# Third batch's score visits regrouped into six PSUM banks, and the last tile's output written in two halves, in a fused attention and MLP kernel

## The chip, the cores and the metric

The kernel runs on one core of one Trainium2 chip. The metric is device time in microseconds of one execution. Before the change the median of 3 runs is 351.26 us (351.23 to 351.55).

## What is computed

Causal attention with 16 extra "beacon" keys per head, then a mixer layer. Batch 8, 8 heads, 576 tokens, head size 64, so 512 channels; the MLP is 512 to 2048 to 512, applied to 8 x 576 = 4608 rows.

```python
k_all = concat([beacon_k, k], axis=2); v_all = concat([beacon_v, v], axis=2)
scores = q @ k_all.T / sqrt(D)            # causal over the 576 tokens, the beacons are open to all
a = softmax(scores); x = a @ v_all        # -> (8, 576, 512)
h = x.T @ U @ V                           # rank 32, along the tokens
u = x + h.T
out = u + relu(u @ w_ch1) @ w_ch2
```

## The kernel before

**Units of work.** Attention runs over 32 *pairs* p of heads: batch `b = p // 4`, pair `c = p % 4` in the batch. Pairs 8 to 11 are the third batch (b = 2). The MLP runs over 9 blocks of 512 rows. Matmul operands are fp16.

For one pair these steps are done, each a short run of instructions:

- *regroup* (`regroup`, L268 and L270, called by `regroup_of`, L691): three VectorE copies that bring the loaded keys (`pr0`) and then the queries (`pr1`) of a pair into the layout that the transposes take.
- *transposes* (`qkT_of`, `qkT_units`): six transposes of the queries into one PSUM bank (TensorE, L275), which a VectorE copy takes to `qT` (L308); the same for the keys, with a second small copy for the beacons (L308, L313).
- *score groups*: the causal score matrix (keys on partitions, queries on columns) of one head is cut into four groups of at most 496 columns, each one bank: group 0 has 496 columns, group 1 464, group 2 496 in three matmuls (336, 80, 80), group 3 208. The two heads of a pair use the two halves of TensorE's rows. A *visit* is a run of such matmuls (L348 in `score_units`, L382 in the freer `visit`), followed by ScalarE's exponentials, which empty the banks into `expt` tiles (L354, L388). There are four `expt` tiles, so pairs p and p + 2 share theirs.
- *masks* (`mask_head`): two VectorE operations per head that cut the causal corners of `expt` (L324, L326). They come after the pair's exponentials and before its value products.
- *value products* (`av_unit`): 15 matmuls per head into one bank `po` (L397), then VectorE's reciprocal (L405) and multiply (L406).

The MLP is a queue of units, four TensorE matmuls of 512 columns each: `g_unit` (L534, `gps`, one bank, emptied at once by ScalarE L547 or VectorE L549, by a fixed rule on the unit's number) and `c_unit` (L560, `cps`; four units share a bank, the last one is followed by VectorE's L573 or, in the first block, L575 and L577, and by the output write). `fill(n)` takes n units from the queue.

**Order.** The order of TensorE, ScalarE, VectorE, SP and POOL is written out by hand: each engine runs its instructions in the order in which the program emits them. PSUM has eight banks; `pst` (L105) hands out the bank that was freed longest ago in the order of the program, and `emptying` (L112) puts a bank at the end of that list when its last reader is emitted. A tile so waits for whichever engine empties its bank.

**The stage of the change.** The main loop (L1007) goes over pairs 8 to 31. Pairs 12 to 31 use `long_slot` (L964), whose visits take six banks and run across pair borders. Pairs 8 to 11 use the general order at its end: visit of groups 0 and 1 of the next pair, first value product, query transposes two pairs ahead, visit of groups 2 and 3 of the next pair, its masks, key transposes, second value product, regroup three pairs ahead. `QUOTA` (L748) spreads 4 MLP units over these steps. Ahead of the loop, pair 8 has its own two visits. Together with pair 8's, the loop makes ten visits of four banks for pairs 8 to 12.

**The last tile.** The last 128 rows of the output are computed by `c_piece` (L581): 256 columns in 16 matmuls, then 128, then 128 columns (L589), each with a VectorE add (L594) and a write on SP's queue (L596).

Of the kernel before, what the change touches and what calls it, by code (L numbers as in the profile page):

```python
# [18 lines left out]
P = 128  # L19
# [11 lines left out]
def kernel(  # L31
# [73 lines left out]
    def pst(shape, dtype, name):  # L105

        b = emptied.pop(0)
        t = psum.tile(shape, dtype, tag=f"bank{b}", name=name)
        bank_of[id(t)] = (b, t)
        return t  # L110
# [407 lines left out]
    def mlp_units(t0, n, dst, flip, turned=True, last=False):  # L518


        units = []
        gT = {}
        held = {}

        def turn():
            ut = utp.tile([P, 4, DM], F16, name="ut", tag="ut")
            for cc in range(NCC):
                nc.sync.dma_start_transpose(out=ut[:, :, ts(cc, P)], in_=uT[:, cc, ds(t0, 4 * P)])
            gT["u"] = ut

        def g_part(dc, upto):
            g, done = held.get(dc) or (pst([P, 512], F32, name="gps"), 0)
            for cc in range(done, upto):
                nc.tensor.matmul(  # L534
                    g[:, 0:n], w1[:, cc, ts(dc, P)], uT[:, cc, ds(t0, n)], start=(cc == 0), stop=(cc == NCC - 1)
                )
            held[dc] = g, upto

        def g_unit(dc):
            if dc == 0:  # L540
                gT["t"] = gtp.tile([P, NDC, 512], F16, name="gT", tag="gT")
                if turned:
                    turn()
            g_part(dc, NCC)
            g, _ = held.pop(dc)
            if (dc % 3 if not turned else (dc + flip) % 2 or dc in (5, 6, 7)):
                nc.scalar.activation(out=gT["t"][:, dc, 0:n], in_=g[:, 0:n], func=AF.Relu)  # L547
            else:
                nc.vector.tensor_scalar_max(out=gT["t"][:, dc, 0:n], in0=g[:, 0:n], scalar1=0.0)  # L549
            emptying(g)  # L550

        cps = {}

        def c_unit(i, part):
            m = min(P, n - P * i)
            if part == 0:
                cps["t"] = pst([P, DM], F32, name="cps")
            ps = cps["t"]
            for dc in range(4 * part, 4 * part + 4):
                nc.tensor.matmul(  # L560
                    ps[:m, :], gT["t"][:, dc, ds(P * i, m)], w2[:, dc, :], start=(dc == 0),
                    stop=turned and dc == NDC - 1, skip_group_check=True,
                )
            if part == 3:
                ob = outp.tile([P, DM], F32, name="ob", tag="ob")
                if not turned:
                    for cc in range(NCC):
                        nc.tensor.matmul(
                            ps[:m, ts(cc, P)], uT[:, cc, ds(t0 + P * i, m)], ident, start=False, stop=True,
                            skip_group_check=True,  # L570
                        )
                if turned:
                    nc.vector.tensor_tensor(out=ob[:m, :], in0=ps[:m, :], in1=gT["u"][:m, i, :], op=ALU.add)  # L573
                elif i % 2:
                    nc.scalar.activation(out=ob[:m, :], in_=ps[:m, :], func=AF.Copy)  # L575
                else:
                    nc.vector.tensor_copy(out=ob[:m, :], in_=ps[:m, :])  # L577
                emptying(ps)
                nc.sync.dma_start(out=dst(i, m), in_=ob[:m, :])

        def c_piece(i, part):  # L581

            o, w, d0, d1 = [
                (0, 2 * P, 0, NDC // 2), (0, 2 * P, NDC // 2, NDC), (2 * P, P, 0, NDC), (3 * P, P, 0, NDC)
            ][part]
            if d0 == 0:
                cps["t"] = pst([P, w], F32, name="cph")
            for dc in range(d0, d1):
                nc.tensor.matmul(  # L589
                    cps["t"], gT["t"][:, dc, ts(i, P)], w2[:, dc, ds(o, w)], start=(dc == 0), stop=(dc == NDC - 1)  # L590
                )
            if d1 == NDC:
                ob = outp.tile([P, w], F32, name="oh", tag="ob")
                nc.vector.tensor_tensor(out=ob, in0=cps["t"], in1=gT["u"][:, i, ds(o, w)], op=ALU.add)  # L594
                emptying(cps["t"])
                nc.sync.dma_start(out=dst(i, P)[:, ds(o, w)], in_=ob)  # L596

        units += [lambda dc=dc: g_unit(dc) for dc in range(NDC)]
        for i in range((n + P - 1) // P):
            c = c_piece if last and i == n // P - 1 else c_unit  # L600
            units += [lambda i=i, part=part, c=c: c(i, part) for part in range(4)]
        return units, g_part

# [87 lines left out]
    def regroup_of(p):  # L691
        b, c = divmod(p, NH2)
        prs[p] = [regroup(Ls[b][0], c, i, nc.vector.tensor_copy) for i in range(2)]
# [15 lines left out]
    def qkT_of(p):  # L709
        b, c = divmod(p, NH2)  # L710
        new_qT_of(p)
        copies = [(act_copy, nc.vector.tensor_copy) if p == 0 else (nc.vector.tensor_copy,)] * 2
        turns = by_heads(Ls[b][0], c)
        for i, t in enumerate(prs.get(p, ())):
            if t is not None:
                turns[i] = in_pair(prs[p])[i]
        return qkT_units(turns, qTs[b], kTs[b % 2], c, copies, Ls[0][0][0] if p == 0 else None)
# [4 lines left out]
    def scores_of(p):  # L722
        b, c = divmod(p, NH2)
        return score_units(c, qTs[b], kTs[b % 2], expts_of(p), p in ON_PE)

    def masks_of(p):
        scores_of(p)[2]()

    def av_of(p):
        b, c = divmod(p, NH2)  # L730
        if c == 0:
            xbs[b] = xbp.tile([P, NT, DM], F16, name="xb", tag="xb")
        return [
            lambda i=i: av_unit(b, 2 * c + i, expts[(2 * p + i) % NE], vss[b % 2], xbs[b]) for i in range(2)
        ]


    NF = 2
# [5 lines left out]
    HINT = 5  # L744

    FIRST = [3, 3, 2, 1]

    QUOTA = {2: 4}  # L748

    IDLE = [8, 1, 1, 0, 1]  # L750
    queue = []
# [7 lines left out]
    def fill(n):  # L759
        while n > 0 and queue:  # L760
            u = queue.pop(0)
            if u is not None:
                u()
            n -= 1
# [28 lines left out]
    with tc.manual_schedule(engines={ENG.PE, ENG.Activation, ENG.DVE, ENG.SP, ENG.Pool}):  # L793
# [135 lines left out]
        regroup_of(NP1)  # L929
        regroup_of(NP1 + 1)  # L930
        fill(8)
        t0, sc, t1 = qkT_of(NP1), scores_of(NP1), qkT_of(NP1 + 1)
        for u in t0 + sc[0:1] + t1[0:1] + sc[1:3] + t1[1:2]:
            u()
            fill(1)
        regroup_of(NP1 + 2)
        tr = []


# [10 lines left out]
        def go(parts, mixed=0):  # L950

            parts = [(p, g) for p, g in parts if p < NP]
            if parts:
                visit(parts)
            for u in mixing[:mixed]:
                u()
            del mixing[:mixed]
# [6 lines left out]
        def long_slot(p, c, av, qk):  # L964
# [29 lines left out]
            else:  # L994
# [6 lines left out]
                if p + 1 < NP:  # L1001
# [2 lines left out]
                    masks_of(p + 1)  # L1004
                    fill(1)

        for p in range(NP1, NP):  # L1007
            b, c = divmod(p, NH2)
            if c == (1 if b >= DT0 else 0) and b + 1 < B:
                load_batch(b + 1)  # L1010
            if c == (1 if b + 1 == DT0 else 2) and DT0 <= b + 2 < B:
                load_whole(b + 2)
            sc = scores_of(p + 1) if p < P6 else []
            qk = qkT_of(p + 2) if p + 2 < min(NP, DT0 * NH2) else []
            av = av_of(p) if p < P6 else []
            if c == 0 and DT0 <= b + 1 < B and b != DT0:
                tr = turns(b + 1)
            if c == NH2 - 1 and b + 1 == DT0:
                tr = turns(b + 2)
            if c in (0, NH2 - 1) and b + 1 == DT0:  # L1020
                fill_turns(tr, NT)
            if c == 0 and b > NF and p <= P6:
                (mix if p < P6 else mix_between)(b - 1)
            if c == 0 and b + 1 >= DT0:
                fill_turns(tr, 2 * NT)
            if p >= P6:
                long_slot(p, c, av_of(p), qk or [lambda: None] * 2)
                continue
            seq = sc[0:1] + av[0:1] + qk[0:1] + sc[1:3] + qk[1:2] + av[1:2]
            if p + 3 < min(NP, DT0 * NH2):  # L1030
                seq.append(lambda p=p: regroup_of(p + 3))
            quota = QUOTA.get(b, 9)
            done = 0
            for i, u in enumerate(seq):
                want = quota * (i + 1) // len(seq)
                if p + 1 == P6 and i + 1 == len(seq):
                    fill(want - done)
                    done = want
                u()
                fill(want - done)  # L1040
                done = want
        mix(B - 1)
        guard()

# [106 lines left out]
```

## Time and profile before

| what | value |
|---|---|
| median of 3 runs | 351.26 us |
| the profiled execution's own time | 351.05 us |
| its span, first to last instruction | 349.4 us |
| granted TensorE clock, mean | 0.998 |
| busy TensorE / VectorE / ScalarE / POOL | 98% / 54% / 47% / 28% |
| first visit of pair 8 / first visit of pair 13 | 62.41 us / 93.02 us |
| last matmuls of the last tile | from 341.55 us for 3.55 us |

The profile is of one execution. Times in it count from the span's start. A line number is that of the kernel before; where a helper makes an instruction, it is the helper's. "Idle before, releaser" tells what ended the time in which an engine stood still. Matmuls overlap each other by their pipeline, so a group's listed length is longer than the distance to the next group.

### The profile page before, as it was taken

Reading aid. Unit: us, or ns where it says so; the run is one execution under the profiler, and the core shown is the slowest. Engines: PE = TensorE matmul, PEld = TensorE weight load, DVE = VectorE, ACT = ScalarE, POOL = GpSimd, SP = SyncE. Lnnn points to the kernel's source line nnn. Section 1 sums busy time; section 2 is a strip of 40 time slices with the busy share of each in tenths; the row PEclk is TensorE's granted clock in tenths of the full one; section 3 lists DMA queues with packets and bytes.
Section 4 is the critical chain, followed back from the end, with each engine's and each line's share of the span. In section 5 each row is a group of like instructions: output and inputs, shape, how many; then the busy total and the mean of one; then the engine's idle time right before and its main releaser. Section 6 shows DMA issues by size and latency. Waiting matters only on the chain.

```text
span 349.4 us, 7841 instructions
## 1 busy us (share of the span) xinstructions
PE 342.7 (98%) x3105; PEld 174.1 (50%) x3105; DVE 190.2 (54%) x494; ACT 164.2 (47%) x359; POOL 97.9 (28%) x137
## 2 busy tenths in 40 slices
PE   8999999999999999999999999999999999999995
PEld 4565565455554445545454454445445444444444
DVE  5766865588976554645565455535564643323311
ACT  5967851587831666167524843485335103202400
POOL 8976715327415437401840050000000000000000
PEclk9999999999999999999999999999999999999999
DMA  9999999999997999991999899533121323013011
GB/s 167 134 191 174 171 205 171 226 142 142 105 132 136 171 139 125 152 213 29 127 136 157 174 95 134 138 95 68 62 90 32 61 99 90 2 60 105 18 64 65
DMA packets 146780, 41.89 MB, mean 120 GB/s; under 512 B 131504, under 2 KB 142224, under 8 KB 146736
## 3 DMA queue, kind: packets, MB, share of 16 engines
q0 software_dynamic: 87440, 18.18, 66.8%
q1 hardware_dynamic: 59072, 22.84, 37.0%
q8 instruction: 26, 0.43, 0.5%
q10 hardware_dynamic: 224, 0.30, 0.3%
q14 instruction: 18, 0.15, 0.1%
HBM read 37.37 MB, written 9.44 MB: 134 GB/s over the span
## 4 chain that ended last, share of the span: by engine, by line
PE 95%; ACT 2%; DVE 1%; issue 0%
PE gps L534 36%; PE cps L560 35%; PE po L397 8%; PE sps L382 5%; PE sps L348 3%; ACT expt L354 2%; PE tps L275 1%; PE idle L250 1%; PE cph L589 1%; PE qtp L434 1%; PE tps L281 1%; PE ups L459 1%; PE ups L413 1%; DVE qT L308 0%; PE qtp L489 0%; DVE kT L308 0%
## 5 line engine op out<-in xcount | busy, mean ns | idle before, releaser
L534 PE MATMUL gps<-uT,w 128*128 128x512 f16 x576 | 135.7, 379 | 0.1
L560 PE MATMUL cps<-w,gT 128*128 128x512 f16 x560 | 130.6, 379 | 0.0
L388 ACT ACTIVATE expt<-sps 128x496 f16<-128x496 f32 (+2 forms) x152 | 65.3, 537 | 63.9 <-PE sps L382 63.9
L547 ACT ACTIVATE gT<-gps 128x512 f16<-128x512 f32 x86 | 51.8, 619 | 79.8 <-PE gps L534 78.0
L534 PEld LDWEIGHTS <-w 128*128 128x128 f16 x576 | 51.6, 98 | 58.5 <-issue 4.2
L560 PEld LDWEIGHTS <-gT 128*128 128x128 f16 x560 | 51.0, 98 | 57.7 <-issue 3.9
L549 DVE TENSOR_SCALAR gT<-gps 128x512 f16<-128x512 f32 x58 | 40.1, 691 | 43.6 <-PE gps L534 41.9
L354 ACT ACTIVATE expt<-sps 128x496 f16<-128x496 f32 (+1 forms) x104 | 44.7, 589 | 6.7 <-PE sps L348 6.7
L573 DVE TENSOR_TENSOR ob<-cps,ut 128x512 f32<-128x512 f32 x31 | 21.4, 690 | 44.1 <-PE cps L560 43.4
L218 POOL DMA_DIRECT2D vs<-in_v_dram x50 | 39.6, 811 | 15.7 <-DMA w<-in_moe_w_ch_dram 5.9
L397 PEld LDWEIGHTS <-expt 128*128 128x128 f16 (+1 forms) x960 | 36.4, 98 | 14.4 <-issue 2.2
L397 PE MATMUL po<-vs,expt 128*128 128x65 f16 (+1 forms) x960 | 39.4, 194 | 0.1
L406 DVE TENSOR_TENSOR xb<-po,rec 128x320 f16<-128x320 f32 x64 | 31.4, 491 | 2.2
L324 DVE TENSOR_TENSOR expt<-expt,bigmask 128x512 f16<-128x512 f16 x58 | 24.2, 417 | 14.0 <-ACT expt L388 12.4
L405 DVE RECIPROCAL rec<-po 128x5 f32<-128x5 f32 x64 | 12.0, 188 | 22.8 <-PE po L397 22.7
L200 POOL DMA_DIRECT2D vs<-in_beacon_v_dram x8 | 4.3, 536 | 58.1 <-PE po L397 58.1
L382 PE MATMUL sps<-qT,kT 64*128 64x496 f16 (+2 forms) x228 | 18.5, 281 | 0.0
L649 POOL DMA_DIRECT2D st<-in_q_dram x20 | 16.9, 869 | 2.7 <-DMA vs<-in_v_dram 1.4
L649 POOL DMA_DIRECT2D st<-in_k_dram x20 | 16.9, 875 | 1.9 <-DMA vs<-in_v_dram 1.9
L446 DVE TENSOR_TENSOR uT<-ups,uT 128x496 f16<-128x496 f32 x24 | 14.5, 667 | 3.9 <-PE ups L459 3.1
L382 PEld LDWEIGHTS <-kT 64*128 64x128 f16 x228 | 7.9, 94 | 14.6 <-issue 11.9
L348 PE MATMUL sps<-qT,kT 64*128 64x80 f16 (+3 forms) x156 | 14.0, 282 | 0.7 <-DVE qT L308 0.6
(97 smaller groups left out, 169.3 us busy)
## 6 DMA issues: line engine op xcount, KB each, us to landing
out_dram<-ob SPq DMA_DIRECT2D x35, 256.0 KB, 2.5
vs<-in_v_dram POOLq DMA_DIRECT2D x18, 128.0 KB, 7.9
w<-in_moe_w_ch_dram POOLq DMA_DIRECT2D x4, 512.0 KB, 6.1
w<-in_moe_w_ch_dram POOLq DMA_DIRECT2D x2, 1024.0 KB, 13.4
st<-in_k_dram POOLq DMA_DIRECT2D x12, 128.0 KB, 7.4
st<-in_q_dram POOLq DMA_DIRECT2D x12, 128.0 KB, 10.9
st<-in_k_dram POOLq DMA_DIRECT2D x2, 576.0 KB, 12.9
st<-in_q_dram POOLq DMA_DIRECT2D x2, 576.0 KB, 15.7
```

What stands on the lines that cost most here:

```text
L218: nc.gpsimd.dma_start(out=dst[a : a + nq[j], j, :, :], in_=src[hs, ds(q0[j], nq[j]), :].rearrange("h p d -> p h d"))
L348: nc.tensor.matmul(ps[g, i][:, ds(o, w)], kT[hp, c, ds(P * ch, P)], qT[hp, c, ds(qa, w)], start=not early, stop=True, skip_group_check=early,)
L354: nc.scalar.activation(out=ex[i][:, ds(SLOT * g, gw[g])], in_=ps[g, i][:, 0 : gw[g]], func=AF.Exp, scale=scale)
L382: nc.tensor.matmul(ps[p, g, i][:, ds(o, w)], kT[hp, c, ds(P * ch, P)], qT[hp, c, ds(qa, w)], start=True, stop=True,)
L388: nc.scalar.activation(out=at[p][3][i][:, ds(SLOT * g, gw[g])], in_=ps[p, g, i][:, 0 : gw[g]], func=AF.Exp, scale=scale)
L397: nc.tensor.matmul(po[:, j, :], ex[0 : nk[c], ds(blk[(c, j)], P)], vs[0 : nk[c], ds(c * H * E + h * E, E)], start=(c == 0), stop=(c == j),)
L406: nc.vector.tensor_tensor(out=xb[:, :, ds(h * D, D)], in0=po[:, :, 0:D], in1=r.broadcast_to([P, NT, D]), op=ALU.mult)
L534: nc.tensor.matmul(g[:, 0:n], w1[:, cc, ts(dc, P)], uT[:, cc, ds(t0, n)], start=(cc == 0), stop=(cc == NCC - 1))
L547: nc.scalar.activation(out=gT["t"][:, dc, 0:n], in_=g[:, 0:n], func=AF.Relu)
L549: nc.vector.tensor_scalar_max(out=gT["t"][:, dc, 0:n], in0=g[:, 0:n], scalar1=0.0)
L560: nc.tensor.matmul(ps[:m, :], gT["t"][:, dc, ds(P * i, m)], w2[:, dc, :], start=(dc == 0), stop=turned and dc == NDC - 1, skip_group_check ...
L649: nc.gpsimd.dma_start(out=dst[a : m[j], j, :, :], in_=src[:, ds(q0[j], nq[j]), :].rearrange("h p d -> p h d"))
```

## The change

In the third batch, the general order is replaced by a hand-written `slot` for each of the pairs 8 to 11. Its visits take six banks (three score groups of both heads) and run across pair borders: (8: 0, 1), then (8: 2, 3; 9: 0), (9: 1, 2, 3), (10: 0, 1, 2), (10: 3; 11: 0, 1), (11: 2, 3; 12: 0), (12: 1, 2, 3). That makes seven visits. All of them use `visit` (L382). The masks, transposes, value products and regroups are emitted at other places between them, and 22 MLP units instead of 23 are emitted before the fourth batch's first visit. In the last tile, the second 256 columns are computed and written as one piece, in 16 matmuls instead of 32.

```diff
-        def c_piece(i, part):
-            o, w, d0, d1 = [
-                (0, 2 * P, 0, NDC // 2), (0, 2 * P, NDC // 2, NDC), (2 * P, P, 0, NDC), (3 * P, P, 0, NDC)
-            ][part]
...
+        def c_half(i, part):
+            hs = ds(DM // 2 * (part // 2), DM // 2)
+            if part % 2 == 0:
+                cps["t"] = pst([P, DM // 2], F32, name="cph")
+            for dc in range(NDC // 2 * (part % 2), NDC // 2 * (part % 2 + 1)):
...
+            if part % 2:
+                ob = outp.tile([P, DM // 2], F32, name="oh", tag="ob")
+                nc.vector.tensor_tensor(out=ob, in0=cps["t"], in1=gT["u"][:, i, hs], op=ALU.add)
...
-        t0, sc, t1 = qkT_of(NP1), scores_of(NP1), qkT_of(NP1 + 1)
-        for u in t0 + sc[0:1] + t1[0:1] + sc[1:3] + t1[1:2]:
+        t0, t1 = qkT_of(NP1), qkT_of(NP1 + 1)
+        for u in t0 + [lambda: visit([(NP1, 0), (NP1, 1)])] + t1:
             u()
             fill(1)
         regroup_of(NP1 + 2)
+        visit([(NP1, 2), (NP1, 3), (NP1 + 1, 0)])
+        fill(1)
...
+        def slot(p, c, av, qk):
+            if c == 0:
+                qk[0]()
+                fill(1)
+                masks_of(p)
+                qk[1]()
+                fill(1)
+                go([(p + 1, 1), (p + 1, 2), (p + 1, 3)])
+                fill(1)
+                weighted(av, 0, 0)
+                regroup_of(p + 3)
+                fill(1)
+            elif c == 1:
+                qk[0]()
+                fill(1)
+                masks_of(p)
+                go([(p + 1, 0), (p + 1, 1), (p + 1, 2)])
+                fill(1)
+                qk[1]()
+                weighted(av, 1, 0)
+                regroup_of(p + 3)
+                fill(1)
+            elif c == 2:
+                go([(p, 3), (p + 1, 0), (p + 1, 1)])
+                fill(1)
+                qk[0]()
+                masks_of(p)
+                fill(1)
+                weighted(av[0:1] + qk[1:2] + av[1:2], 0, 0, 0)
+                regroup_of(p + 3)
+                fill(1)
+            else:
+                go([(p, 2), (p, 3), (p + 1, 0)])
+                fill(1)
+                qk[0]()
+                fill(1)
+                masks_of(p)
+                qk[1]()
+                fill(1)
+                go([(p + 1, 1), (p + 1, 2), (p + 1, 3)])
+                fill(1)
+                weighted(av, 0, 0)
+                masks_of(p + 1)
+                fill(1)
+                regroup_of(p + 3)
...
-            if p >= P6:
-                long_slot(p, c, av_of(p), qk or [lambda: None] * 2)
-                continue
-            seq = sc[0:1] + av[0:1] + qk[0:1] + sc[1:3] + qk[1:2] + av[1:2]
-            if p + 3 < min(NP, DT0 * NH2):
-                seq.append(lambda p=p: regroup_of(p + 3))
-            quota = QUOTA.get(b, 9)
...
+            (slot if p < P6 else long_slot)(p, c, av_of(p), qk or [lambda: None] * 2)
```

Here `av` are the two value products of pair p, `qk` the query and the key transposes of pair p + 2 with their copies, `go(parts)` a visit, `weighted(units, n...)` runs units with n MLP units behind each.

More of the change, by code (lines that the diff above doesn't have):

```diff
@@ L579, in c_unit @@
                 nc.sync.dma_start(out=dst(i, m), in_=ob[:m, :])
-        def c_piece(i, part):
-            o, w, d0, d1 = [
-                (0, 2 * P, 0, NDC // 2), (0, 2 * P, NDC // 2, NDC), (2 * P, P, 0, NDC), (3 * P, P, 0, NDC)
-            ][part]
-            if d0 == 0:
-                cps["t"] = pst([P, w], F32, name="cph")
-            for dc in range(d0, d1):
+        def c_half(i, part):
[3 more added lines that the diff above has]
+            for dc in range(NDC // 2 * (part % 2), NDC // 2 * (part % 2 + 1)):
                 nc.tensor.matmul(
-                    cps["t"], gT["t"][:, dc, ts(i, P)], w2[:, dc, ds(o, w)], start=(dc == 0), stop=(dc == NDC - 1)
+                    cps["t"], gT["t"][:, dc, ts(i, P)], w2[:, dc, hs], start=(dc == 0), stop=(dc == NDC - 1)
                 )
-            if d1 == NDC:
-                ob = outp.tile([P, w], F32, name="oh", tag="ob")
-                nc.vector.tensor_tensor(out=ob, in0=cps["t"], in1=gT["u"][:, i, ds(o, w)], op=ALU.add)
+            if part % 2:
+                ob = outp.tile([P, DM // 2], F32, name="oh", tag="ob")
+                nc.vector.tensor_tensor(out=ob, in0=cps["t"], in1=gT["u"][:, i, hs], op=ALU.add)
                 emptying(cps["t"])
-                nc.sync.dma_start(out=dst(i, P)[:, ds(o, w)], in_=ob)
+                nc.sync.dma_start(out=dst(i, P)[:, hs], in_=ob)
         units += [lambda dc=dc: g_unit(dc) for dc in range(NDC)]
         for i in range((n + P - 1) // P):
-            c = c_piece if last and i == n // P - 1 else c_unit
+            c = c_half if last and i == n // P - 1 else c_unit
             units += [lambda i=i, part=part, c=c: c(i, part) for part in range(4)]
@@ L746 @@
     FIRST = [3, 3, 2, 1]
-    QUOTA = {2: 4}
     IDLE = [8, 1, 1, 0, 1]
@@ L1012 @@
                 load_whole(b + 2)
-            sc = scores_of(p + 1) if p < P6 else []
             qk = qkT_of(p + 2) if p + 2 < min(NP, DT0 * NH2) else []
-            av = av_of(p) if p < P6 else []
             if c == 0 and DT0 <= b + 1 < B and b != DT0:
@@ L1021 @@
                 fill_turns(tr, NT)
-            if c == 0 and b > NF and p <= P6:
-                (mix if p < P6 else mix_between)(b - 1)
+            if p == P6:
+                mix_between(b - 1)
             if c == 0 and b + 1 >= DT0:
                 fill_turns(tr, 2 * NT)
-            if p >= P6:
-                long_slot(p, c, av_of(p), qk or [lambda: None] * 2)
-                continue
-            seq = sc[0:1] + av[0:1] + qk[0:1] + sc[1:3] + qk[1:2] + av[1:2]
-            if p + 3 < min(NP, DT0 * NH2):
-                seq.append(lambda p=p: regroup_of(p + 3))
-            quota = QUOTA.get(b, 9)
[L1033 to L1041, printed above, removed]
+            (slot if p < P6 else long_slot)(p, c, av_of(p), qk or [lambda: None] * 2)
         mix(B - 1)
```

## The prediction, made before the changed kernel was run

> **What bounds the kernel now.** I read, in this order, the page's busy table, the waits of TensorE, the PE timeline of the third batch (visits between 62.4 and 93.0 us), the DVE timeline of the same stretch, and the last ten microseconds with their DMA issues.
>
> ```profile
> PE 342.7 (98%) x3105; PEld 174.1 (50%) x3105; DVE 190.2 (54%) x494; ACT 164.2 (47%) x359; POOL 97.9 (28%) x137
> ```
> ```profile
> PE sps L348 <- DVE qT L308: 0.6, 2, 0.3
> ```
>
> TensorE is the bound: apart from the start, hardly anything makes it wait (0.6 us in two places, both early). So a microsecond of TensorE saved is a microsecond gained, and a wait put on TensorE is lost in full. The PE timeline (start, length, operation):
>
> ```profile
> 80.91 0.58 PE L348 MATMUL sps<-qT,kT 64*128 64x496 f16 x4
> 81.42 0.62 PE L397 MATMUL po<-vs,expt 128*128 128x65 f16 x15
> 81.89 1.03 PE L534 MATMUL gps<-uT,w 128*128 128x512 f16 x4
> 82.75 0.42 PE L275 MATMUL tps<-ident,pr 96*128 96x96 f16 x6
> 83.11 0.48 PE L348 MATMUL sps<-qT,kT 64*128 64x336 f16 x8
> 83.52 1.03 PE L534 MATMUL gps<-uT,w 128*128 128x512 f16 x4
> ```
>
> Lengths overlap, so I count from start to start: a unit of four MLP products is 0.86 (81.89 to 82.75), one head's value products (po) 0.46, six transposes 0.27 where an MLP unit follows (84.39 to 84.66), but 0.36 where a score visit follows (82.75 to 83.11). An MLP unit ahead of a visit is 0.96 (79.95 to 80.91). So **entering a visit costs 0.10**. The visit at 80.91 streams 496 + 464 columns, its two heads side by side; 512 columns take 0.215, so these should take 0.40, and they take 0.51. The visit at 83.11 has 704 columns, 0.30, and takes 0.41. The six-bank visit at 112.63, 1168 columns or 0.49, takes 0.60. So **leaving costs 0.11 whatever the size**.
>
> The DVE timeline, one pair's work of the same stage:
>
> ```profile
> 84.59 0.69 DVE L549 TENSOR_SCALAR gT<-gps 128x512 f16<-128x512 f32 x1 [0.62 <-PE gps L534]
> 85.20 0.41 DVE L324 TENSOR_TENSOR expt<-expt,bigmask 128x512 f16<-128x512 f16 x1
> 85.53 0.19 DVE L326 TENSOR_TENSOR expt<-expt,mask 80x80 f16<-80x80 f16 x1
> ...
> 86.09 0.75 DVE L308 COPY kT<-tps 128x576 f16<-128x576 f16 x1
> 86.75 0.15 DVE L313 COPY kT<-tps 128x16 f16<-128x16 f16 x1
> 86.83 0.18 DVE L405 RECIPROCAL rec<-po 128x5 f32<-128x5 f32 x1
> 87.04 0.49 DVE L406 TENSOR_TENSOR xb<-po,rec 128x320 f16<-128x320 f32 x1
> 87.45 0.35 DVE L268 COPY pr<-st 96x768 f16<-96x768 f16 x1
> 87.81 0.19 DVE L270 COPY pr<-st 16x128 f16<-16x128 f16 x1
> 88.01 0.35 DVE L268 COPY pr<-st 96x768 f16<-96x768 f16 x1
> 88.29 0.68 DVE L549 TENSOR_SCALAR gT<-gps 128x512 f16<-128x512 f32 x1
> ```
>
> From it, by starts: MLP eviction 0.61 (0.69 to its end), the four masks 0.89 (0.41 to the first one's end), key copy 0.66 plus 0.08, reciprocal and multiply 0.62, regroup 0.84 (0.91 to its end). VectorE has 4.5 to 5.4 us of work in each 6.05 us pair: it is covered, but every piece has a place in one fixed queue. Hand-overs: po ends at 81.89 and its reciprocal starts at 82.09, so TensorE to VectorE is 0.20; L313 ends at 62.34 and the visit starts at 62.41, so the way back is 0.07.
>
> **The change, part by part.** Three visits fewer at 0.10 + 0.11: **-0.63 us**; columns and exponentials are the same. One MLP unit (22 instead of 23 ahead of the fourth batch) moves later, and its 0.86 with it: nothing by itself.
>
> The new order puts VectorE results closer to their use. I went through the printed order of each engine with the durations above, keeping which PSUM bank each tile takes. Four places come out late, in time order:
>
> 1. Pair 8 to pair 9. Both heads' value products now come together, then the regroup of pair 11, one MLP unit, and at once the query transposes of pair 11, which need that regroup. (Now a further visit, a unit and a value product stand between.) From the end of the MLP unit after the visit of pair 9, VectorE has: 0.20 hand-over, eviction 0.61, two reciprocal and multiply 1.24, regroup 0.91, back 0.07 = 3.03. TensorE has 0.46 + 0.46 + 0.86 = 1.78. **Wait 1.25.**
> 2. Pair 10. Its visit's first two banks are its last group, so the masks come after it, behind the query copy of pair 12, with one MLP unit of cover before the value products. From the transposes' end: 0.20 + 0.66 + 0.41 + 0.07 = 1.34 against 0.86. **Wait 0.48.**
> 3. Pair 11's start. The query transposes of pair 13 take the bank of an MLP unit whose eviction stands behind the regroup of pair 13. From the end of pair 10's first value product: 0.20 + 0.62 + key copy 0.74 + 0.62 + 0.84 + 0.69 + 0.07 = 3.78. TensorE: transposes 0.27, po 0.46, unit 0.86, visit 0.10 + 0.61, unit 0.86 = 3.16. **Wait 0.62.**
> 4. Pair 11's second visit. The MLP unit behind it takes the bank of the key transposes of pair 13, whose copy stands behind an eviction and the masks: 0.20 + 0.61 + 0.89 + 0.66 + 0.15 + 0.07 = 2.58, against 0.27 + 0.86 + 0.10 + 0.61 = 1.84. **Wait 0.74.**
>
> Sum +3.09. Elsewhere the banks come free in time: the tightest are 0.35 us (the unit after pair 9's visit) and a few tenths behind the six exponentials, of which six-bank visits from 93.02 on already show that TensorE doesn't wait for them. In the batches after, the unit order is shifted by one: evictions change engine, but their banks are needed at least 0.4 us after they come free. I take 0, with +0.3 as the upper end. The queues of POOL and SP keep their order. **Stage: -0.63 + 3.09 = +2.46**; bounds +1.3 (waits 1 and 2, the shortest chains, and a little of the others) to +3.3.
>
> The last tile:
>
> ```profile
> 343.34 0.42 DVE L594 TENSOR_TENSOR oh<-cph,ut 128x256 f32<-128x256 f32 x1 [1.05 <-PE cph L589]
> ...
> 345.12 0.29 DVE L594 TENSOR_TENSOR oh<-cph,ut 128x128 f32<-128x128 f32 x1 [0.60 <-PE cph L589]
> ```
> ```profile
> out_dram<-oh SPq DMA_DIRECT2D x1, 128.0 KB, 1.7
> out_dram<-oh SPq DMA_DIRECT2D x2, 64.0 KB, 2.7
> ```
>
> Two quarter columns of sixteen matmuls take 0.89 each (344.23 to 345.12), a half 1.74: 0.04 less. The last add is 0.42 where it was 0.29: +0.13. The last write, 64 KB, is issued at 345.44 and lands 2.8 later; the half-width write, the same size that the change would issue last, took 1.7. That is -1.1 if it repeats, 0 if whatever slows the very last write stays (its issue on SP took 1.28, others 0.33). I take 1.7, as the row of the same shape: **-1.0 in all**, with +0.1 as the other end.
>
> **Sum:** +2.46 - 1.01 = +1.45. The profiled execution took 351.05 (span 349.4), 0.2 below the median of 351.26; so about 352.5 against its own time and **352.7** against the median.
>
> **Rivals.**
> - *VectorE catches up (faster).* If VectorE's spare 0.7 to 1.5 us a pair were what counts, not the order, no wait would show: -0.63 - 1.01 = -1.6, or 349.6. It decides at wait 1: the regroup of pair 11 would have to end within 1.7 us of that MLP unit, not 3.0. Against it: four operations stand ahead of it in a strict queue, two of which wait for products just ended. Chance 0.12.
> - *Half the waits.* Waits 3 and 4 follow from banks and long chains; with 1.3 to 2 us of waits in all, the result is -0.3 to +0.4, 351.0 to 351.7, within the bound. 0.13.
> - *The tail gives nothing.* +2.46 + 0.1: 353.8. Inside my forecast's range; I hold it nearly as likely as 1.0 less.
> - *The clock falls in a wait.* The eight matmuls at the start take 0.45 each (3.60 us on the chain) where later ones take 0.215. One such stretch more would cost 3.6 x (1 - 0.215/0.45) = 1.9: 354.6. Against it: the PEclk row is 9 from slice 1 to 40. [...] With the shifted units waiting in each of five batches (5 x 0.3 = 1.5) it shares 0.08.
> - *The change doesn't do what it says.* The printed order shows seven visits and 32 matmuls for 48 in the last tile; 0.02.
>
> The forecast has 0.65, from 351.9 to 354.3 (stage +1.7 to +3.0, tail -1.0 to 0). With the neighbours, 8 in 10 lies in **351.4 to 354.4**. A difference of 0.2%, 0.7 us, is about what can be told from no change. Slower 0.74, same 0.13, faster 0.13.
>
> **What would show it.** In the changed profile: TensorE's waits list L275 and L397 and L534 waiting for VectorE (pr L268, expt L324, gT L549, kT L313), 3 us in all between 70 and 92 us; visits still 0.60 for 1168 columns; from 96 on the batches again 36.27 apart (130.43 to 166.7 now); a last write landing within 2 us. If TensorE shows no wait of about 1.2 us ahead of the query transposes of pair 11, the forecast is wrong.

## The result, and the profile after

The changed kernel takes 353.97 us (353.18 to 354.97, 6 runs) where the kernel before takes 351.37. The ratio is 1.0074, 95% interval 1.0063 to 1.0084: **0.74% slower**, 2.6 us. The prediction was 352.7, in a range of 351.4 to 354.4. The profiled execution took 354.19, its span is 352.4 us, 3.0 more than before.

The waits of TensorE in the changed kernel (who waited for whom: us in total, times, longest):

```profile
PE tps L275 <- DVE pr L268: 1.9, 3, 1.1
...
PE gps L534 <- DVE kT L313: 0.7, 1, 0.7
PE sps L348 <- DVE qT L308: 0.6, 2, 0.3
PE tps L275 <- DVE gT L549: 0.4, 1, 0.4
PE po L397 <- DVE expt L324: 0.3, 1, 0.3
...
```

Of these, only the `qT` line was there before. The others are new, and in all of them TensorE waits for VectorE: for a regroup (`pr`), for the key copy, for an MLP eviction, for a mask. Of the 1.9 us of the first line, 1.1 lies in the third batch. The rest is two short waits at 4.8 and 5.9 us, far ahead of anything the change touches; they come and go from profile to profile. The list counts from the listed end of the group before (73.00 + 1.03 = 74.03, which is 1.10 ahead of 75.13); what the next unit lost is read from starts in the PE timeline:

```profile
62.55 0.58 PE L382 MATMUL sps<-qT,kT 64*128 64x496 f16 x4
...
73.00 1.03 PE L534 MATMUL gps<-uT,w 128*128 128x512 f16 x4
75.13 0.43 PE L275 MATMUL tps<-ident,pr 96*128 96x96 f16 x6 [1.10 <-DVE pr L268]
...
80.96 0.67 PE L382 MATMUL sps<-qT,kT 64*128 64x208 f16 x6
81.56 1.04 PE L534 MATMUL gps<-uT,w 128*128 128x512 f16 x4
82.75 0.43 PE L275 MATMUL tps<-ident,pr 96*128 96x96 f16 x6
83.01 1.03 PE L534 MATMUL gps<-uT,w 128*128 128x512 f16 x4
84.36 0.62 PE L397 MATMUL po<-vs,expt 128*128 128x65 f16 x15 [0.32 <-DVE expt L324]
...
87.16 1.04 PE L534 MATMUL gps<-uT,w 128*128 128x512 f16 x4
88.59 0.42 PE L275 MATMUL tps<-ident,pr 96*128 96x96 f16 x6 [0.39 <-DVE gT L549]
...
90.94 0.67 PE L382 MATMUL sps<-qT,kT 64*128 64x464 f16 x10
92.28 1.04 PE L534 MATMUL gps<-uT,w 128*128 128x512 f16 x4 [0.67 <-DVE kT L313]
...
96.16 1.04 PE L534 MATMUL gps<-uT,w 128*128 128x512 f16 x4
```

A unit of four MLP products takes 0.87 from start to start. So the transposes at 75.13 are 1.26 late (73.00 + 0.87 = 73.87), those at 82.75 0.32, the value product at 84.36 0.48, the transposes at 88.59 0.56, and the MLP unit at 92.28 0.74 (the visit ahead of it needs 0.60, as the one at 80.96 shows). Together with 0.04 ahead of the unit at 87.16 that is 3.40 us.

The stage as a whole runs from the first visit of pair 8 to the first unit behind the fourth batch's `qtp` (L434, the matmuls with U that open the mixer of a batch). Its two ends before the change:

```profile
62.41 0.58 PE L348 MATMUL sps<-qT,kT 64*128 64x496 f16 x4
...
94.24 1.02 PE L560 MATMUL cps<-w,gT 128*128 128x512 f16 x4
```

That is 31.83; after, 62.55 to 96.16, it is 33.61, with one MLP unit of 0.86 less in it. So it is 33.61 + 0.86 - 31.83 = **2.64 us longer**. If the visits gave back 0.63 of the 3.40, 2.77 is left; 0.13 is not accounted for. Behind the stage a batch again takes 36.28 (`qtp` at 133.08 and 169.36; before 131.15 and 167.42, 36.27). In this execution 0.25 more went in the sixth batch, in one visit that took 0.87 and not 0.62 (at 193.91).

### The profile page after: what moved, and what is told of

It reads as the page before. It is cut to its first block, busy times and chain, and to the rows that moved or that the text cites. A ratio compares the mean times of both kernels' runs of the same rounds, so it can differ in the third digit from the quotient of the medians.

```text
span 352.4 us, 7808 instructions
## 1 busy us (share of the span) xinstructions
PE 342.3 (97%) x3089; PEld 173.0 (49%) x3089; DVE 191.2 (54%) x493; ACT 164.1 (47%) x359; POOL 97.6 (28%) x137
## 4 chain that ended last, share of the span: by engine, by line
PE 90%; DVE 5%; ACT 2%; DMA 1%; issue 0%
PE cps L560 35%; PE gps L534 34%; PE po L397 8%; PE sps L382 5%; ACT expt L354 2%; PE sps L348 1%; PE tps L275 1%; PE cph L586 1%; DMA stq<-in_q_dram 1%; DVE pr L268 1%; DVE xb L406 1%; PE qtp L434 1%; DVE kT L308 1%; PE tps L281 1%; DVE qT L308 1%; PE ups L459 1%
## 5 line engine op out<-in xcount | busy, mean ns | idle before, releaser
L388 ACT ACTIVATE expt<-sps 128x496 f16<-128x496 f32 x192 | 82.5, 536 | 73.8 <-PE sps L382 73.8
L547 ACT ACTIVATE gT<-gps 128x512 f16<-128x512 f32 x86 | 51.0, 624 | 80.5 <-PE gps L534 78.7
L549 DVE TENSOR_SCALAR gT<-gps 128x512 f16<-128x512 f32 x58 | 39.9, 690 | 43.3 <-PE gps L534 41.7
L324 DVE TENSOR_TENSOR expt<-expt,bigmask 128x512 f16<-128x512 f16 x58 | 24.1, 416 | 6.7 <-ACT expt L388 6.7
L354 ACT ACTIVATE expt<-sps 128x496 f16<-128x496 f32 (+1 forms) x64 | 27.0, 612 | 0.7 <-PE sps L348 0.6
L382 PE MATMUL sps<-qT,kT 64*128 64x80 f16 (+4 forms) x288 | 23.5, 281 | 0.1
L382 PEld LDWEIGHTS <-kT 64*128 64x128 f16 x288 | 10.0, 94 | 18.5 <-issue 15.1
L308 DVE COPY qT<-tps 128x576 f16<-128x576 f16 (+1 forms) x16 | 11.8, 737 | 5.3 <-PE tps L275 3.2
```

The costliest lines, as they stand in the source:

```text
L324: nc.vector.tensor_tensor(out=e4, in0=e4, in1=bigmask, op=ALU.min)
L354: nc.scalar.activation(out=ex[i][:, ds(SLOT * g, gw[g])], in_=ps[g, i][:, 0 : gw[g]], func=AF.Exp, scale=scale)
L382: nc.tensor.matmul(ps[p, g, i][:, ds(o, w)], kT[hp, c, ds(P * ch, P)], qT[hp, c, ds(qa, w)], start=True, stop=True,)
L388: nc.scalar.activation(out=at[p][3][i][:, ds(SLOT * g, gw[g])], in_=ps[p, g, i][:, 0 : gw[g]], func=AF.Exp, scale=scale)
```

## The experiments

Each was timed against the kernel before, on the same chip; medians of before were 351.3 to 351.5. "Stage" is the length just defined, with the moved unit left out (after: 33.61; before would be 30.97).

**The last tile alone.** The kernel before, with `c_half` in place of `c_piece`:

```diff
-            c = c_piece if last and i == n // P - 1 else c_unit
+            c = c_half if last and i == n // P - 1 else c_unit
```

> The kernel before with the last tile's two halves alone. Theory A (the row that the prediction took: a last half-width write lands in 1.7 us): 1.0 us faster than before, 350.3. Theory B (the end takes what it takes after the last add, 4.0 us before and 3.9 after, whatever the width): within 0.2 us of before, 351.2 to 351.6.

Measured: 351.14 against 351.38, ratio 0.9996 (0.9981 to 1.0012). Theory A is out: 1.0 us would be 0.9972. From the last add's end to the span's end it is 3.6 us, where before had 4.0. The first of the two half-width writes landed 2.6 us after its issue, the last one 2.2. In the changed kernel they show as

```profile
out_dram<-oh SPq DMA_DIRECT2D x2, 128.0 KB, 2.5
```

with 2.6 for the first and 2.4 for the last, and 3.9 us from the last add to the end. The 1.7 that the prediction took came again only at its old place: in the two other profiles with three pieces the first write, half as wide as the tile, also landed in 1.7. As the last write it took 2.1 to 2.4 in all eight profiles with two halves. The trace has sixteen completions for each write. In all eight, fifteen of the last write's sixteen came within 1.7 us, and only the sixteenth was late (in the changed kernel 1.55 to 1.70, then 2.44). What held it back is not shown. From the last landing to the end of the span it is 1.4 us in all eleven profiles.

**The third batch alone.** The changed kernel, with `c_piece` again:

```diff
-            c = c_half if last and i == n // P - 1 else c_unit
+            c = c_piece if last and i == n // P - 1 else c_unit
```

> The changed kernel with the last tile in three pieces again, so the third batch's new order alone. Theory (the stage costs +2.6 and the tail gives 0.0 to 0.3): 2.5 to 2.9 us slower than the kernel before, 353.9 to 354.3. Rival (the tail's two halves cost the end something that the last add and write hide): 353.5 or less.

Measured: 354.17 against 351.46, ratio 1.0067 (1.0047 to 1.0087). The stage is 33.60. So the loss is in the third batch's order, to within the interval's 0.7 us either way.

**The regroup of pair 11 earlier**, all else as changed:

```diff
                 qk[1]()
+                regroup_of(p + 3)
                 fill(1)
                 go([(p + 1, 1), (p + 1, 2), (p + 1, 3)])
                 fill(1)
                 weighted(av, 0, 0)
-                regroup_of(p + 3)
                 fill(1)
```

> The changed kernel with the regroup of pair 11 emitted ahead of the visit of pair 9, into VectorE's idle 1.4 us there; nothing else differs. Theory (the wait at the query transposes of pair 11, about 1.3 us, is the regroup's place in VectorE's queue): that wait is gone and the kernel is 1.0 to 1.3 us faster than the changed one, 352.7 to 353.0. Rival (the six-bank visits or the shifted units cost the time, and TensorE's wait there would move to the next place): less than 0.4 us faster, 353.6 to 354.0, with a new wait of about 1 us behind it.

Measured: 352.40, ratio 1.0034 (1.0019 to 1.0048), 1.6 us below the changed kernel's median. The stage is 32.00, 1.61 less: the 1.26 is gone, and so is the 0.32 at the transposes of pair 12, whose regroup now ends at 81.19, before TensorE is ready for it at 81.46. The waits for L549 and L313 are still there with 0.4 and 0.7.

**The other places.** Pair 10's masks ahead of the query copy, regroups of pairs 12 and 13 a step earlier, pair 11's masks behind the key copy:

```diff
                 go([(p + 1, 0), (p + 1, 1), (p + 1, 2)])
+                regroup_of(p + 3)
                 fill(1)
                 qk[1]()
                 weighted(av, 1, 0)
-                regroup_of(p + 3)
+                regroup_of(p + 4)
...
-                qk[0]()
                 masks_of(p)
+                qk[0]()
                 fill(1)
                 weighted(av[0:1] + qk[1:2] + av[1:2], 0, 0, 0)
-                regroup_of(p + 3)
...
-                masks_of(p)
                 qk[1]()
+                masks_of(p)
```

> The changed kernel with pair 10's masks ahead of the query copy of pair 12, the regroups of pairs 12 and 13 a step earlier, and pair 11's masks behind the key copy of pair 13; the regroup of pair 11 stays late. Theory (waits 2 to 4, with the slow regroup of pair 12, make up about 1.7 to 2.0 us): 352.0 to 352.4 with TensorE's first wait of 1.2 us left. Rival (these three are the first wait's aftermath): 353.5 to 354.0, with waits in the same places.

Measured: 351.62, ratio 1.0017 (1.0001 to 1.0033), 2.3 us below the changed kernel and 0.4 below the theory's lower end. The stage is 31.48, 2.13 less; 0.32 + 0.48 + 0.56 + 0.04 + 0.74 is 2.14. In the third batch, the first wait of 1.1 is left alone. So these waits are not the first one's aftermath.

**Pair 11's masks behind the key copy, alone** (the last hunk above):

> The changed kernel with pair 11's masks behind the key copy of pair 13 instead of ahead of it. Theory (the MLP unit after pair 11's second visit waits 0.7 for the bank of that copy): that wait is gone, 0.7 us faster than the changed kernel, 353.2 to 353.4, the other waits as they were. Rival (the copy is late for another reason, or the masks are then late for the value products): no gain, with a wait of about 0.7 at the value products of pair 11.

Measured: 352.92, ratio 1.0037 (1.0024 to 1.0051). The wait for L313 is gone from the list, and the waits for the regroup of pair 11, the mask and L549 are as they were; the stage is 32.87, 0.74 less. That it equals the wait is in part chance: the transposes of pair 12 are only 0.11 late here, 0.21 less than in the changed kernel, and transposes at 68.12 are 0.21 late that were not late there. The medians differ by 1.05, the spans of the two profiled executions by 0.7; the changed kernel's runs are 1.8 us apart, and where the rest lies is not settled.

**All four places mended** (both edits above together):

> Both edits together. Theory: no wait of TensorE on VectorE over 0.2 us between pairs 8 and 12 is left, so the three saved visits show: 0.4 to 0.7 us faster than the kernel before, 350.7 to 351.0. Rival (six-bank visits cost something of their own in this stage): 351.4 or more, without a wait in the list that accounts for it.

Measured: 350.54 (350.30 to 351.00, 12 runs), ratio **0.9977 (0.9966 to 0.9987)**: faster than both kernels. What is left of TensorE's waits on other engines is the list of before:

```profile
PE idle L250 <- DVE ones L153: 1.2, 1, 1.2
PE sps L348 <- DVE qT L308: 0.6, 2, 0.3
PE sps L340 <- ACT expt L354: 0.2, 1, 0.2
```

The stage is 30.45, 0.52 less than the 30.97 of before; the rest of the 0.84 between the medians is about what the last tile gave. One unit (at 80.59) is still 0.2 late, for a bank that VectorE's multiply empties behind the slow regroup of pair 12.

**The price of a visit.** In the kernel before, five visits more:

```diff
-                go([(p + 1, 0), (p + 1, 1), (p + 1, 2)], 1)
+                go([(p + 1, 0), (p + 1, 1)])
                 fill(1)
+                go([(p + 1, 2)], 1)
```

> The kernel before with one more visit in each of the five later batches: the six-bank visit at the start of a batch makes its third group after one MLP unit instead of at once; columns, exponentials and units are the same. Theory (a visit costs 0.10 to enter and 0.11 to leave): 1.05 us slower, 352.4. Rival (the 0.21 is pipeline fill that the next group would hide anyway): within 0.2 us of before.

Measured: 352.38 against 351.46, ratio 1.0026 (1.0013 to 1.0039), 0.5 to 1.4 us. The PE timeline of this kernel, at the first of them:

```profile
93.90 0.58 PE L382 MATMUL sps<-qT,kT 64*128 64x496 f16 x4
94.41 1.04 PE L560 MATMUL cps<-w,gT 128*128 128x512 f16 x4
95.38 0.39 PE L382 MATMUL sps<-qT,kT 64*128 64x336 f16 x6
95.70 0.47 PE L434 MATMUL qtp<-xb,Usb 112*32 112x128 f16 x20
```

The unit takes 0.97 ahead of a visit, the two visits 0.51 and 0.32, together 0.83, where one visit of the same columns took 0.72. A batch takes 36.49 (`qtp` at 133.23 and 169.72), 0.22 more than before. Of the five added visits, four cost 0.20 to 0.22 in the trace and the one in the second of these batches 0.12 (93.74 to 131.15 before, 95.70 to 133.23 here); together 0.98.

**POOL's loads later.** All four places mended, and `load_whole(4)` emitted a pair later:

```diff
-            if c == (1 if b + 1 == DT0 else 2) and DT0 <= b + 2 < B:
+            if c == (1 if b + 1 == DT0 else 3 if b + 2 == DT0 else 2) and DT0 <= b + 2 < B:
```

> The kernel with all four places mended, and the ten loads of batch 4's queries and keys issued by POOL one pair later, so that they no longer stand beside the regroups of pairs 12 and 13. Theory (a regroup copy that meets a load issue of POOL takes up to 0.7 instead of 0.35 and 0.19): these regroups take 0.35, 0.19 and 0.36 again, and the 0.2 that TensorE loses at the transposes of pair 12 goes: 350.2 to 350.5, unless the later landing makes SP's transposes of batch 4 late. Rival (the regroups of pairs 12 and 13 are slow for a reason of their own): they keep their 0.68 and 0.70, and the time stays.

Measured: 350.60, ratio 0.9976 (0.9962 to 0.999), as without the edit. It tells nothing of its theory: POOL had nothing else to do and issued the loads at 71.9 us all the same, as soon as the regroup of pair 11 had freed their tile. The copies stayed at 0.67 and 0.70.

**The regroups moved out of the loads' way instead:**

```diff
                 qk[1]()
+                regroup_of(p + 4)
                 regroup_of(p + 3)
...
                 weighted(av[0:1] + qk[1:2] + av[1:2], 0, 0, 0)
                 fill(1)
+                regroup_of(p + 3)
```

(the first in pair 8, the second in pair 10; pair 9 has none).

> As the kernel with all four places mended, but with the regroup of pair 12 in front of that of pair 11, which POOL's loads of batch 4 wait for, and the regroup of pair 13 behind pair 10's last MLP eviction. So the regroups of pairs 12 and 13 stand before and after those loads. Theory (a regroup copy is slow only beside a load issue of POOL): the regroups of pairs 11 to 13 take 0.35, 0.19 and 0.36 each, and the 0.2 at the transposes of pair 12 goes; a wait of about 0.4 at the query transposes of pair 13 may come, as its regroup is now late: 350.3 to 350.9. Rival (these regroups are slow for a reason of their own, the third batch's busy VectorE for one): copies of 0.64 to 0.70 are still among them.

Measured: 351.06 against 351.34, ratio 0.9997 (0.9985 to 1.001). The loads ran from 72.3 to 82.9. The regroup of pair 13 behind them:

```profile
85.40 0.35 DVE L268 COPY pr<-st 96x768 f16<-96x768 f16 x1
85.76 0.19 DVE L270 COPY pr<-st 16x128 f16<-16x128 f16 x1
85.97 0.36 DVE L268 COPY pr<-st 96x768 f16<-96x768 f16 x1
```

Those of pairs 11 and 12, from 70.65 on, took the same. The unit and the transposes of pair 12 are no longer late. As expected, the transposes of pair 13 now are, by 0.56 (86.38, where 84.95 + 0.87 = 85.82), and the stage is 30.78. So the theory of the slow copies came out as forecast, though it was the copies that were moved here and not the loads. The stage is still 0.33 longer than in the order before it, and the median is 0.2 above the forecast's upper end.

## Why the prediction was right, and where it was off

- **TensorE is the bound, and what is put on it is lost in full**: right. The sum of its late starts less the visits, 3.40 - 0.63 = 2.77, is close to the stage's 2.64. The stage had been forecast at 2.46.
- **A visit costs 0.21**: right. Five more cost 0.98 in the trace, where 1.05 was forecast, and with the waits taken away the three fewer show as a stage 0.52 shorter.
- **Wait 1**: 1.25 predicted, 1.26 measured, and shown to be the regroup's place in the queue: moved into VectorE's idle time, it goes. **Wait 2**: 0.48 and 0.48. **Wait 3**: 0.62, and 0.56 with 0.04 ahead of it. **Wait 4**: 0.74 and 0.74, shown by moving one mask call. Waits 2 and 3 were only taken away together with wait 4; that each has the predicted cause rests on the rows, where the named VectorE result ends just ahead of TensorE's start.
- **Left out**: 0.32 at the transposes of pair 12. Their regroup had been costed at 0.91 from a row taken at 87 us. The profile of before already had slow ones: 0.71 and 0.67 for two copies at 94.10 and 95.03. Here it took 1.85, from 80.83 to 82.68:

```profile
80.83 0.75 DVE L268 COPY pr<-st 96x768 f16<-96x768 f16 x1
81.62 0.68 DVE L270 COPY pr<-st 16x128 f16<-16x128 f16 x1
82.33 0.35 DVE L268 COPY pr<-st 96x768 f16<-96x768 f16 x1
```

- **The last tile, -1.0**: this is the step that failed. The two halves take 0.04 less on TensorE and the last add 0.13 more, as said; but the landing, put at -1.1, was wrong at both ends. The last write of before landed 2.6 us after its issue; the 2.8 is the second write's. And the last half-width write landed in 2.1 to 2.4 and not 1.7, by its sixteenth completion. "The row of the same shape" was a single write with two more behind it. So the landing gave 0.4 in the profile of the last tile alone and 0.1 in that of the changed kernel, and the sign that the prediction named, a last write within 2 us, did not come. The measured worth of this part is -0.24 us in the medians, within the uncertainty of nothing. With 0 in its place the sum would have been 353.7.
- **The range** held without luck in the sum: the last tile and the regroup left out miss in the same direction, and no large errors cancelled. Of the single numbers, the one for a tail that gives nothing, 353.8, came closest to the 353.97.
- **The rivals**: VectorE did not catch up, though it was busy for 191.2 of 352.4 us. TensorE's granted clock did not fall in waits of up to 1.26 us: its mean is 1.000, and its row on the page shows 9 in all 40 slices. The 0.5 that the traces of the two kernels do show lies inside the last slice, behind the last matmul: 2.6 us after its end before (345.1 to 347.7), 4.2 after (348.1 to 352.3). No wait of TensorE in the changed kernel is that long. The shifted units cost nothing in the later batches but the 0.25 at 193.91. The same visit took 0.97 in the profile with pair 11's masks moved alone, and 0.62 in the nine others, of which six also have the shifted units; its cause is open.

## What to carry to other kernels

When an order is written by hand for the engine that is full, walk through the queue of the half-busy engine too: a result is late by what stands ahead of it in its own queue, whatever that engine's average (the transposes of pair 11 by 1.26 us, with VectorE 54% busy). Keep long copies that a later step needs at the place where their engine is idle, as the regroup of pair 11 in the changed kernel's idle stretch of VectorE between 70.9 and 72.3 us, and put work that frees a bank ahead of work that nobody waits for yet, as the key copy ahead of pair 11's masks (0.74 us less in the stage). A tail estimated from one short write is worth its whole range (1.7 to 2.8 us in the profile of before), not its best row.

## What the runs showed of the hardware

The regroup copies run on VectorE from SBUF to SBUF. In ten profiles (before, after, and the first eight experiments), between 30 and 105 us, 106 copies of L268 (96 x 768, fp16) and L270 overlap no load issue of POOL, and none of them takes over 0.36 and 0.19 us. Of the 164 that do overlap one, 66 take over 1.3 times that, up to 0.76 and 0.70; what spares the others is not shown. The slow copies just shown stood beside these issues:

```profile
79.67 4.23 POOL L646 DMA_DIRECT2D st<-in_q_dram  x5
```

The masks (L324 and L326, two inputs) took the same beside POOL and away from it, 0.41 to 0.43 and 0.19 us, and so did the copies out of PSUM (L308), 0.74 to 0.76 (149 and 136 of them overlapped an issue). So of these three kinds only the regroup copies were slowed, and only beside an issue. What slows them is not shown.
